# Attention and mixture of experts: the second products of the jobs of 448 and 360 columns change from row form to column form

## The chip, the cores and the metric

The program runs on one core of one Trainium2 chip. The metric is the device time of one launch in microseconds. The kernel before takes 369.8 us, the median of three runs (368.93 to 370.06).

## The reference

A gated linear attention gives one row of 384 values for each of 3072 tokens. A gate sends each token to one of eight experts, and each expert is a network of two layers. The change touches only the experts:

```python
expert_idx = np.argmax(x @ w_gate, axis=1)
...
h = np.maximum(np.einsum('ecd,edf->ecf', disp, w1), 0.0)
y = np.einsum('ecf,efd->ecd', h, w2)
...
out[i] = gate_w[i] * y[expert_idx[i], pos[i]]
```

Here D is 384 and F is 1024, so that one expert has a first product of 384 by 1024 and a second of 1024 by 384.

## The kernel before

The first 145 us or so are the attention. Its rows go to a scratch tensor in HBM, `disp`, sorted by expert. Then nine jobs run one after the other. Jobs 0 and 1 are the tokens of expert 0 (256 and 224 of them). Jobs 2 to 8 are the other experts, sorted by their number of tokens and padded to fixed sizes. In the branch that this input takes, the sizes are `T_USUAL`: 448, 424, 408, 392, 376, 360 and 352. A second branch with larger sizes (`T_SORTED`) is in the program and doesn't run.

Every job multiplies in pieces: an operand is split into a high part (`hh`, `xh`, `w1h`, `w2h`) and a rest (`hl`, `xl`, `w1l`, `w2l`), and three matmuls, high by high, rest by high and high by rest, make one product. The steps of a job are:

- `load_rows` (L1188, L1192) brings the job's rows `xg` from `disp`. `columns` (L1199) splits their words into two planes of 16 bits on POOL (L1206) and ACT (L1207), and SP issues one DMA transpose for each block of 128 rows (L1210), which gives `xq`. `prep_columns` (L1215) puts the planes together again (L1219 on POOL, L1220 on ACT) as `x` and splits `x` into `xh` (ACT, L1224) and `xl` (DVE, L1225). One buffer of `xh` and `xl` serves all jobs.
- `ffn1` (L1289) is the first product: for each of eight `ft`, nine matmuls (L762) with the job's T columns moving, into one bank of PSUM. `hidden_out` evicts it as `hh` (ACT, L768) and `hl` (DVE, L769).
- the second product has two forms. **Row form**, `ffn2_rows` (L1013): for each block of 128 tokens, 24 matmuls (L1023) whose stationary operand is 128 (or fewer) tokens of `hh` or `hl`, and whose moving operand is the 384 columns of `w2`. A last block of 64 tokens moves 384 columns too. ACT evicts each block with the gate as scale (`yo`, L1027), and POOL scatters its rows to the output (L334). **Column form**, `ffn2` (L1304): for each `ft` and each of three groups of 128 output features, three matmuls (L1312) whose stationary operand is `w2` and whose moving operand is the T tokens; three banks of PSUM fill together. Their result has features on the partitions, so ACT (L1318) and DVE (L1319) evict it as two planes of 16 bits, `yp`, and SP issues three DMA transposes to `yq` (L1320). In the first product of the next job, `emit_out` (L1326) puts the words together (POOL, L1332, and ACT, L1333), multiplies by the gate (ACT, L1334) and scatters.
- the weights of the next job are loaded by SP into a ring of three buffers (`raw`, L129 and L133) and split by ACT (L140) and DVE (L149; four pieces of job 2 on POOL).

`IN_ROWS` (L67) names the jobs whose second product is in row form. The rest of the loop decides by it too: after a job in row form `hook` is `None`, after one in column form it is the call of `emit_out`. Two more places hang on it:

```python
        nc.gpsimd.memset(yp[:, :, :, min(sizes[j - 2] for j in range(2, NE + 1) if j not in IN_ROWS) :], 0)
...
            if j == len(jobs) - 1:
                with tc.issue_after(out_ins[-1]):
                    nc.gpsimd.drain()
```

The second (L1373 to L1375) issues a drain of POOL behind the last scatter that `out_ins` knows. Only `ffn2_rows` appends to `out_ins`; the scatters of `emit_out` don't.

In the jobs from 2 on, the scheduler of the framework orders the instructions of each engine, from the dependences, the order of the code and its own model. Each engine takes its queue in order; SP's queue issues the loads and the transposes.

Of the kernel before, what the change touches and what calls it, by code (L numbers as in the profile page):

```python
# [29 lines left out]
def kernel(  # L30
# [33 lines left out]
    T_SORTED = (480, 440, 424, 408, 396, 384, 368)  # L64
    T_USUAL = (448, 424, 408, 392, 376, 360, 352)
    TMAX = max(T_SORTED)
    IN_ROWS = (0, 1, 2, 7, 8)  # L67
    NS = NE - 1
    XW = 2 * D + NE
    TOK0 = 4096  # L70
# [942 lines left out]
    def ffn2_rows(wt, hs, pr, T, fpool, hooks=None, fills=True):  # L1013
        w1h, w1l, w2h, w2l = wt
        gate, ti = pr[2:]
        for kb in range(-(-T // P)):
            n = min(P, T - kb * P)
            ks = slice(kb * P, kb * P + n)
            py = psM.tile([P, DM], F32, name="psM")
            for ft in range(FT):  # L1020
                hh, hl = hs[ft][:2]
                for m, (x, a) in enumerate(((hh, w2h), (hl, w2h), (hh, w2l))):
                    nc.tensor.matmul(py[:n], x[:, ks], a[:, ft], start=(ft == 0 and m == 0), stop=(ft == FT - 1 and m == 2))  # L1023
                if hooks and (kb, ft) in hooks:
                    hooks[kb, ft]()
            yo = fpool.tile([P, DM], F32, name="yo", bufs=2 if hooks and fills else 3)
            nc.scalar.activation(yo[:n], py[:n], AF.Copy, scale=gate[:n, kb : kb + 1])  # L1027
            with tc.issue_after(filling[-1]) if hooks and fills and kb else ExitStack():
                out_ins.append(scatter(out, ti[:n, kb : kb + 1], yo[:n], N - 1, ("out",)))
# [145 lines left out]
    def sorted_jobs(fctx, sizes):  # L1175
# [23 lines left out]
        def columns(xg, T):  # L1199
            nb, full = -(-T // P), T // P  # L1200
            planes = fpool.tile([P, 4, 2, DM], U16, name="planes", bufs=1)
            xq = fpool.tile([P, 2 * DT, whole(T_SORTED[1])], U16, name="xq", bufs=1)
            words = xg.bitcast(U16)[:, :, : 2 * DM].rearrange("r k (d w) -> r k d w", w=2)
            for r, ks in ((P, slice(0, full)), (whole(T - full * P), slice(full, nb))):
                if ks.start < ks.stop:
                    nc.gpsimd.tensor_copy(planes[:r, ks, 0], words[:r, ks, :, 1])  # L1206
                    nc.scalar.activation(planes[:r, ks, 1], words[:r, ks, :, 0], AF.Copy)  # L1207
            for kb in range(nb):
                r = whole(min(P, T - kb * P))
                nc.sync.dma_start_transpose(  # L1210
                    xq[:, :, kb * P : kb * P + r], planes[:r, kb].rearrange("r w d -> r (w d)")
                )
            return (xq,) + gates(xg, nb, fpool)
# [131 lines left out]
        yp = fpool.tile([P, DT, 2, 4 * P], U16, name="yp", bufs=1)  # L1345
        nc.gpsimd.memset(yp[:, :, :, min(sizes[j - 2] for j in range(2, NE + 1) if j not in IN_ROWS) :], 0)
        xgs, made = {}, {}
# [17 lines left out]
        for j, (_, T, ws) in list(enumerate(jobs))[2:]:  # L1365
# [15 lines left out]
            if j + 2 in xgs:  # L1381
                made[j + 2] = columns(xgs.pop(j + 2), jobs[j + 2][1])
            if j in IN_ROWS:
                ffn2_rows(wsets[ws], hs, cur, T, fpool)
# [207 lines left out]
```

## Time and profile before

| | |
|---|---|
| median of three runs | 369.8 us |
| the profiled execution, its own time | 366.9 us |
| its span, first to last instruction | 365.2 us |
| TensorE clock granted, mean | 0.997 |
| busy PE, DVE, ACT, POOL | 97%, 68%, 61%, 46% of the span |
| instructions | 10100 |

The profiled execution is one run, and its own time lies 0.8% below the median of the timed runs. Busy shares are averages over the attention and the experts. A matmul in the rows lasts about twice the distance to the next one, since two overlap; a price is therefore taken from the starts.

### The profile page before, as it was taken

What the parts mean: (1) busy time and instruction counts of PE and PEld (TensorE: products, weight loads), DVE (VectorE), ACT (ScalarE), POOL (GpSimd) and SP (SyncE); (2) the same over time, 40 slices, a digit from 0 to 9 for tenths busy, and PEclk for the clock granted to TensorE, in tenths of its full rate; (3) what the DMA queues carried; (4) which work ended last, traced back from release to release, by engine and by line L of the source; (5) the groups of instructions that cost most, each with busy time, mean ns of one, the idle gap of its engine ahead of it and who ended that gap; (6) DMA issues with size and microseconds to landing.
All of it is one profiled execution on the core that took longest, in us unless ns stands there. A gap on an engine that the chain in (4) does not pass through costs nothing. (4 is left out here: it accounts for less than half of the span.)

```text
span 365.2 us, 10100 instructions
## 1 busy us (share of the span) xinstructions
PE 355.5 (97%) x3895; PEld 335.1 (92%) x3895; DVE 247.2 (68%) x538; ACT 221.6 (61%) x457; POOL 166.8 (46%) x282
## 2 busy tenths in 40 slices
PE   7999999999999999999999999999999999999993
PEld 7999988888788889999999899999999999999993
DVE  4899997988798866745884576874954956670300
ACT  3356677886686754144677494868758776782310
POOL 6655555585767676241735320314615425073012
PEclk9999999999999999999999999999999999999998
DMA  8999999999999432467396779899599799831001
GB/s 149 197 174 218 216 192 232 244 217 203 230 222 245 132 114 90 135 217 229 115 253 225 194 245 214 254 230 278 162 205 275 173 193 292 167 124 61 14 23 43
DMA packets 110571, 67.54 MB, mean 185 GB/s; under 512 B 92996, under 2 KB 105053, under 8 KB 110513
## 3 DMA queue, kind: packets, MB, share of 16 engines
q1 hardware_dynamic: 106784, 56.74, 70.7%
q0 software_dynamic: 3456, 9.96, 7.9%
q8 instruction: 32, 0.52, 0.7%
q14 instruction: 27, 0.21, 0.2%
q10 hardware_dynamic: 272, 0.10, 0.1%
HBM read 49.26 MB, written 11.21 MB: 166 GB/s over the span
## 5 line engine op out<-in xcount | busy, mean ns | idle before, releaser
L334 POOL DMA_INDIRECT out_dram<-yo,g_ti x29 | 29.8, 1029 | 62.1 <-ACT yo L1027 43.8
L442 POOL TENSOR_SCALAR_AFFINE_SELECT AT<-AT 128x512 f32<-128x512 f32 x48 | 29.5, 640 | 21.0 <-ACT AT L440 20.9
L1023 PE MATMUL psM<-w2h,hh 128*128 128x384 f32 (+3 forms) x112 | 37.7, 341 | 0.0
L1023 PE MATMUL psM<-w2h,hl 128*128 128x384 f32 (+3 forms) x112 | 37.5, 338 | 0.0
L1023 PE MATMUL psM<-w2l,hh 128*128 128x384 f32 (+3 forms) x112 | 37.4, 337 | 0.0
L149 DVE TENSOR_TENSOR w2l<-raw,w2h 128x768 fp32r<-128x768 f32 x28 | 29.6, 1061 | 9.9 <-ACT w2h L140 9.4
L1312 PE MATMUL psM<-hh,w2l 128*128 128x424 f32 (+3 forms) x96 | 33.1, 345 | 0.0
L1312 PE MATMUL psM<-hl,w2h 128*128 128x424 f32 (+3 forms) x96 | 33.0, 344 | 0.0
L1312 PE MATMUL psM<-hh,w2h 128*128 128x424 f32 (+3 forms) x96 | 33.0, 344 | 0.0
L140 ACT ACTIVATE w2h<-raw 128x768 fp32r<-128x768 f32 x32 | 26.7, 842 | 9.6 <-DMA raw<-in_moe_w_dram 8.9
L394 DVE TENSOR_TENSOR_SCAN Suf<-psF,direv 112x511 f32<-112x511 f32 x24 | 29.1, 1210 | 4.5 <-PE psF L374 4.4
L440 ACT ACTIVATE AT<-psA 128x512 f32<-128x512 f32 x48 | 26.4, 613 | 8.9 <-PE psA L434 4.9
L1332 POOL COPY yo<-yq 128x384 uint16<-128x384 uint16 (+4 forms) x15 | 12.7, 898 | 38.4 <-DMA yq<-yp 36.5
L769 DVE SCALAR_TENSOR_TENSOR hl<-psA,hh 128x448 fp32r<-128x448 f32 (+8 forms) x24 | 13.0, 542 | 25.2 <-ACT hh L768 18.9
L434 PE MATMUL psA<-qT,kT 48*128 48x128 f32 x384 | 29.7, 293 | 0.0
L334 POOL DMA_INDIRECT disp<-rows,ri x24 | 24.9, 1036 | 10.1 <-issue 4.3
L408 DVE TENSOR_TENSOR_SCAN Rq<-psF,d 112x512 f32<-112x512 f32 x24 | 29.4, 1224 | 0.0
L140 ACT ACTIVATE w1h<-raw 128x1024 fp32r<-128x1024 f32 x24 | 25.2, 1058 | 4.2 <-DMA raw<-in_moe_w_dram 4.0
L149 DVE TENSOR_TENSOR w1l<-raw,w1h 128x1024 fp32r<-128x1024 f32 x21 | 25.7, 1231 | 2.9 <-ACT w1h L140 2.8
L434 PEld LDWEIGHTS psA<-qT,kT 48*128 48x128 f32 x384 | 26.1, 201 | 0.5 <-issue 0.5
L567 ACT ACTIVATE rows<-psA 128x384 f32<-128x384 f32 x24 | 11.8, 492 | 24.3 <-PE psA L551 18.5
L530 PE MATMUL psY<-AT,ld_v 128*48 128x128 f32 (+1 forms) x384 | 26.0, 273 | 0.0
(270 smaller groups left out, 1033.5 us busy)
## 6 DMA issues: line engine op xcount, KB each, us to landing
raw<-in_moe_w_dram SPq DMA_DIRECT2D x24, 512.0 KB
raw<-in_moe_w_dram SPq DMA_DIRECT2D x32, 384.0 KB
ld_kq<-in_k_dram SPq DMA_DIRECT2D x24, 192.0 KB
ld_kq<-in_q_dram SPq DMA_DIRECT2D x24, 192.0 KB
ld_v<-in_v_dram SPq DMA_DIRECT2D x24, 192.0 KB
ld_f<-in_f_logit_dram SPq DMA_DIRECT2D x11, 384.0 KB
xg<-disp SPq DMA_DIRECT2D x4, 589.5 KB
xg<-disp SPq DMA_DIRECT2D x5, 393.0 KB
```

Of the source, the lines that this page charges most:

```text
L140: return nc.scalar.activation(hi, raw, AF.Copy)
L149: engine.tensor_tensor(lo[cs], raw[cs], hi[cs].bitcast(F32), op=ALU.subtract)
L334: ins = nc.gpsimd.indirect_dma_start(out=dst, out_offset=bass.IndirectOffsetOnAxis(ap=idx, axis=0), in_=rows, in_offset=None, bounds_check ...
L394: nc.vector.tensor_tensor_scan(out=_view(Suf[:R], m - 1, [[-1, m]]), data0=_view(F, m, [[-1, m]]), data1=_view(direv[:R], m - 1, [[-1, m]] ...
L408: nc.vector.tensor_tensor_scan(out=Rq[:R], data0=F, data1=d1[:R], initial=0.0, op0=ALU.mult, op1=ALU.max)
L434: nc.tensor.matmul(pas[s][:, p], kTs[n][r, p], qTs[n][r, p], start=True, stop=True)
L440: nc.scalar.activation(AT[:, s], pas[s], AF.Copy)
L442: nc.gpsimd.affine_select(AT[:, s], AT[:, s], pattern=[[0, NP], [1, C]], compare_op=ALU.is_ge, fill=0.0, base=0, channel_multiplier=-1)
L530: nc.tensor.matmul(py[b][64 * g : 64 * g + m, a, :], vt[:, 2 * p + s, :m], AT[:, s, p, :], start=(first(n) and a == 0), stop=(a == NP // 2 ...
L769: nc.vector.scalar_tensor_tensor(out=hl[:, :T], in0=ph[:, :T], scalar=0.0, in1=hh[:, :T].bitcast(F32), op0=ALU.max, op1=ALU.subtract)
L1023: nc.tensor.matmul(py[:n], x[:, ks], a[:, ft], start=(ft == 0 and m == 0), stop=(ft == FT - 1 and m == 2))
L1312: nc.tensor.matmul(pys[c][:, :T], a[:, ft, cs], x[:, :T], start=(ft == 0 and n == 0), stop=(ft == FT - 1 and n == 2))
```

## The change

`IN_ROWS` loses jobs 2 and 7. The second product of job 2 (448 tokens) and of job 7 (360 tokens) is then made by `ffn2`, and evicted and scattered by way of `yp`, `yq` and `emit_out`. Jobs 0, 1 and 8 stay in row form.

```diff
     TMAX = max(T_SORTED)
-    IN_ROWS = (0, 1, 2, 7, 8)
+    IN_ROWS = (0, 1, 8)
     NS = NE - 1
```

By L1346 the part of `yp` that is set to zero once begins at column 360 and not at 376. By L1374 the drain of POOL is issued behind the last scatter of job 1 and not of job 7: in the built program it stands directly behind the scatter of job 1's second block, ahead of the fourth `w2l` on POOL.

The ACT queue from the conversion of job 3's rows (`x`, 424 columns) to the first evictions of job 3 (`hh`), before:

```order
L1220 ACTIVATE x_9230<-xq 128x3x424
L1027 ACTIVATE yo<-psM,g_gate 128x384
L1207 ACTIVATE planes<-xg 128x3x384
L1207 ACTIVATE planes<-xg 32x384
L1027 ACTIVATE yo<-psM,g_gate 128x384
...
L140 ACTIVATE w2h<-raw_3470 128x768
L1224 ACTIVATE xh<-x_9230 128x424 x3
L140 ACTIVATE w2h<-raw_3471 128x768
L140 ACTIVATE w2h<-raw_3469 128x768
L1027 ACTIVATE yo<-psM,g_gate 128x384
L140 ACTIVATE w2h<-raw_3470 128x768
L1027 ACTIVATE yo<-psM,g_gate 64x384
```

The same stretch with the change:

```order
L1220 ACTIVATE x_9239<-xq 128x3x424
L1207 ACTIVATE planes<-xg 128x3x384
L1207 ACTIVATE planes<-xg 32x384
...
L140 ACTIVATE w2h<-raw_3470 128x768
L1224 ACTIVATE xh<-x_9239 128x424 x3
L1318 ACTIVATE yp<-psM 128x448
L140 ACTIVATE w2h<-raw_3471 128x768
L1318 ACTIVATE yp<-psM 128x448
L140 ACTIVATE w2h<-raw_3469 128x768
L1318 ACTIVATE yp<-psM 128x448
L140 ACTIVATE w2h<-raw_3470 128x768
```

The four row evictions are gone, two of them from ahead of `xh`, and three pieces of job 3's `w2h` now stand between the column evictions.

SP's queue from the last piece of job 3's `w2` to the first of job 4's `w1` (L129), before:

```order
L133 DMA raw_3470<-in_moe_w_dram 128x2x384
...
L1210 DMA_TRANSPOSE xq<-planes 128x6x128 x3
L1210 DMA_TRANSPOSE xq<-planes 128x6x32
L1188 ISA
L1188 DMA xg<-disp 128x3x393
L1192 ISA
L1192 DMA xg<-disp 16x393
L129 ISA
L129 DMA raw_3471<-in_moe_w_dram 128x1024
```

and with the change:

```order
L133 DMA raw_3470<-in_moe_w_dram 128x2x384
...
L1320 DMA_TRANSPOSE yq<-yp 128x8x128
L1210 DMA_TRANSPOSE xq<-planes 128x6x128 x3
L1210 DMA_TRANSPOSE xq<-planes 128x6x32
L1320 DMA_TRANSPOSE yq<-yp 128x8x128 x2
L1188 ISA
L1188 DMA xg<-disp 128x3x393
L1192 ISA
L1192 DMA xg<-disp 16x393
L129 ISA
L129 DMA raw_3471<-in_moe_w_dram 128x1024
```

The three transposes of job 2's result stand around those of job 4's rows, ahead of the load of job 5's rows and of all weights of job 4.

## Rows read from the trace of the kernel before

**Rows 1.** The page, part 1: busy time, share of the span and instructions of each engine.

```profile
PE 355.5 (97%) x3895; PEld 335.1 (92%) x3895; DVE 247.2 (68%) x538; ACT 221.6 (61%) x457; POOL 166.8 (46%) x282
```

**Rows 2.** Busy time by stretch: job 3's first product, then its second; columns in the first line.

```profile
core 0: us, PE busy (x) PEld busy (x) DVE busy (x) ACT busy (x) POOL busy (x), PEclk, DMA share, GB/s
...
206.00:220.00 14.00, 14.00 (x75) 13.64 (x74) 8.66 (x19) 10.03 (x16) 4.26 (x5) 1.00 0.75 223
220.00:234.00 14.00, 14.00 (x75) 13.64 (x74) 9.29 (x19) 9.05 (x14) 3.57 (x4) 1.00 1.07 261
```

**Rows 3.** Line 1023 in job 2, row form: count, duration ns min/median/max, first and last start.

```profile
L1023 PE MATMUL psM<-w2h,hh x32: 332/333/342, 189.0 to 205.3; 128*128 128x384 f32 x24, 128*64 128x384 f32 x8
...
L1023 PE MATMUL psM<-w2l,hh x32: 333/338/342, 189.3 to 205.7; 128*128 128x384 f32 x24, 128*64 128x384 f32 x8
```

**Rows 4.** Line 1312 in job 3, column form of 424 columns.

```profile
L1312 PE MATMUL psM<-hh,w2h x24: 352/353/358, 219.7 to 233.0; 128*128 128x424 f32 x24
...
L1312 PE MATMUL psM<-hh,w2l x24: 349/357/362, 220.1 to 233.4; 128*128 128x424 f32 x24
```

**Rows 5.** Line 762 in job 7, first product of 360 columns, first and last group.

```profile
L762 PE MATMUL psA<-xh,w1h x9: 320/324/330, 310.9 to 320.7; 128*128 128x360 f32 x9
...
L762 PE MATMUL psT<-xh,w1l x9: 322/326/328, 312.7 to 322.5; 128*128 128x360 f32 x9
```

**Rows 6.** ACT in order of time around job 2's second product: start us, us, what.

```profile
191.78 1.67 ACT L1220 ACTIVATE x<-xq 128x1272 uint16<-128x1272 uint16 x1 [0.95 <-DMA xq<-planes]
195.87 0.58 ACT L1027 ACTIVATE yo<-psM,g_gate 128x384 f32<-128x384 f32 x1 [2.42 <-PE psM L1023]
...
199.26 1.44 ACT L1224 ACTIVATE xh<-x 128x424 fp32r<-128x424 f32 x3
```

**Rows 7.** DVE in order of time: job 3's last xl, job 4's last w1l.

```profile
201.62 0.56 DVE L1225 TENSOR_TENSOR xl<-x,xh 128x424 fp32r<-128x424 f32 x1
...
218.59 1.22 DVE L149 TENSOR_TENSOR w1l<-raw,w1h 128x1024 fp32r<-128x1024 f32 x1
```

**Rows 8.** SP in order of time: job 4's w1, the transposes of job 3's result.

```profile
208.74 1.52 SPq L129 DMA_DIRECT2D raw<-in_moe_w_dram  x3
...
237.90 5.00 SPq L1320 DMA_TRANSPOSE yq<-yp  x3
```

**Rows 9.** The instructions that read or write yq: duration ns min/median/max.

```profile
L1333 ACT ACTIVATE yo<-yq x15: 610/627/651, 245.0 to 322.0; 128x384 uint16<-128x384 uint16 x11, 40x384 uint16<-40x384 uint16 x1, 24x384 uint16<-24x384 uint16 x1, 8x384 uint16<-8x384 uint16 x1
L1332 POOL COPY yo<-yq x15: 615/628/1650, 245.1 to 321.3; 128x384 uint16<-128x384 uint16 x11, 40x384 uint16<-40x384 uint16 x1, 24x384 uint16<-24x384 uint16 x1, 8x384 uint16<-8x384 uint16 x1
```

**Rows 10.** Line 1375, POOL's drain: duration ns min/median/max, first and last start.

```profile
L1375 POOLq DRAIN  x1: 5687/5687/5687, 336.1 to 336.1; - x1
```

**Rows 11.** POOL in order of time, job 8.

```profile
336.33 1.01 POOL L334 DMA_INDIRECT out_dram<-yo,g_ti  x1 [2.97 <-ACT yo L1027]
...
360.59 0.94 POOL L334 DMA_INDIRECT out_dram<-yo,g_ti  x1 [3.20 <-POOLq L1554]
```

**Rows 12.** The page, part 5: the scatters to the output and to the scratch tensor.

```profile
L334 POOL DMA_INDIRECT out_dram<-yo,g_ti x29 | 29.8, 1029 | 62.1 <-ACT yo L1027 43.8
...
L334 POOL DMA_INDIRECT disp<-rows,ri x24 | 24.9, 1036 | 10.1 <-issue 4.3
```

**Rows 13.** Line 1588, the end of the program, POOL's part.

```profile
L1588 POOLq EVENT_SEMAPHORE  x4: 17/17/17, 364.4 to 365.1; - x4
L1588 POOLq DRAIN  x3: 50/107/368, 363.1 to 364.9; - x3
```

**Rows 14.** POOL in order of time where job 2 begins.

```profile
181.12 0.95 POOL L334 DMA_INDIRECT out_dram<-yo,g_ti  x1 [0.16 <-issue]
182.08 1.87 POOL L149 TENSOR_TENSOR w2l<-raw,w2h 128x768 fp32r<-128x768 f32 x1
183.87 1.61 POOL L1206 COPY planes<-xg 128x1152 uint16<-128x1152 uint16 x2
```

**Rows 15.** The instructions that read raw, from 170 us on: DVE's rests of w2.

```profile
L149 DVE TENSOR_TENSOR w2l<-raw,w2h x24: 942/959/2430, 199.5 to 327.5; 128x768 fp32r<-128x768 f32 x24
```

## The prediction

> **What bounds the kernel now.** I read the page's busy times first: PE is busy 97% of the span, the next engine 68% [rows 1]. An average over attention and experts says little, so the second view is the busy time by stretch. In job 3's first product PE is busy 14.00 of 14 us at full clock, and in its second product again, while ACT is busy 10.03 and 9.05 of them and DVE 8.66 and 9.29 [rows 2]. So from job 2 on the time is the number of matmuls times their distance, as long as operands come early enough. The DMA engines are the ones to watch: their mean busy share is 0.75 in the first stretch and 1.07 in the second (over 1, so the count lets packets overlap) [rows 2]. The third view is the tail: after the last matmul come one eviction, one scatter at 360.59 and the end of the program [rows 11, 13].
>
> **What PE saves.** In row form job 2 makes four blocks of 24 matmuls, 96 in all. They start from 189.0 to 205.7, which is 95 distances of 0.176 us: 16.9 us [rows 3]. The last block has 64 tokens and its matmuls are as far apart as the others. In column form there are 72 matmuls of 448 columns. No row shows a second product of 448, so I scale the nearest: job 3's 72 start from 219.7 to 233.4, 0.193 us apart for 424 columns, or 0.455 ns a column [rows 4]; 448 columns are then 0.204 us, and 72 of them 14.7 us. Job 2 saves 2.2 us. Job 7 makes 72 matmuls in either form. In row form they are 0.176 us apart [rows 3]; with 360 columns the first product of the same job has 71 distances between 310.9 and 322.5, 0.163 us each [rows 5]. It saves 72 times 0.0125, 0.9 us by these two rows; if a column costs the same 0.455 ns at 360 as at 424, the distance is 0.164 and the saving 0.85. I take 0.8, since the starts are given to a tenth of a us. Together 3.0 us, between 2.8 and 3.2.
>
> The Trainium skill (TensorE: Matmul & The Clock Gate, Back-to-back issue gap) gives an isolated gap of N/2.4 + 2.5 ns at the full clock. By it the two jobs would save 2.0 and 0.7 us, an estimate of 2.7 in place of 3.0. The rows show larger gaps (176 ns at 384 columns, where the page gives 162), and they decide.
>
> **What is added beside PE.** Per job: six evictions of `yp`, three transposes, then for each block of tokens one POOL copy and two ACT operations, against one ACT eviction for each block. A POOL copy takes 0.63 us and an ACT one 0.63 [rows 9]. Job 2 has four blocks, so ACT gets some 5 us more in job 3's first product, in which it is idle for 4 [rows 2]; its four row evictions of 0.58 [rows 6] are gone from the stretch before. PE doesn't feel ACT being late by two or three us there, because the column form asks for `hh` one `ft` at a time, nine matmuls or 1.7 us apart. For the same reason the weights' pieces that now stand between the column evictions on ACT are early enough. I cost all of this at nothing, and say below what it costs without that cover.
>
> On SP three transposes of a result hold the queue for 5.0 us [rows 8]. In job 3 they stand ahead of all weights of job 4. Job 4's last `w1l` is ready at 219.8 now [rows 7], and job 4 begins 0.2 us behind the last start of job 3, at 233.6 [rows 4]: a lead of 13.8 us. Of it go 2.2 (PE is earlier) and 5 (SP), and 6.6 remain. In job 8 the transposes have no load behind them. Nothing on the path.
>
> **Job 3's start** has the smallest lead. Its last `xl` ends at 202.2 [rows 7] and its first matmul follows the last of job 2 at 205.9 [rows 3], a lead of 3.7 us. With the shorter product 1.5 remain. Two row evictions of 0.58 leave the ACT queue ahead of `xh`, one of which waited 2.42 us for PE [rows 6], so `xh` may come earlier by 1.2 to 3.6 us, unless the next rows' `planes` then wait for their load. That makes a lead of 2.7 to 5.1.
>
> **The drain.** This is the term that I am least sure of. The drain is now issued where job 2 begins. Before, it stood in job 8 and took 5.69 us from 336.1 on [rows 10]; the scatter ahead of it ended at 337.3 [rows 11], so the drain alone took 4.4 us. Nothing waited for it: POOL had no work then. The program's last drain began at 363.1 and took 0.37 us [rows 13], and POOL went on at 364.4 only, so it had 0.9 us to spare. Ahead of the long one were 53 scatters (29 and 24 [rows 12], three that fill, less the last three), between it and the short one three. If a drain pays for the scatters since the last one, it is 4.4/53, 0.083 us each. The new first drain then has 31 behind it and takes 2.6 us; the last has 25, takes 2.1 in place of 0.37, and ends 1.7 us later. Less the 0.9 to spare, **the end comes 0.8 us later**. The bounds are 0 (a last drain is always short) and 4.4 us (it takes 5.69, less 0.37 and 0.9). I take 0.8, as the only value that holds for both rows.
>
> The first drain delays POOL's fourth `w2l` and job 3's `planes`, which followed the scatter at 182.1 and 183.9 [rows 14]. 2.6 us of delay in `planes` go through the transposes to `x` and `xh`, against a lead of 2.7 to 5.1. So nothing, just.
>
> **The sum.** -3.0 + 0.8 = -2.2 us on the profiled execution's own 366.9, which gives 364.7. The median of the timed runs is 369.8; 0.6% less is **367.6 us**.
>
> **The rivals.**
>
> *The last drain is free.* Then the gain is all of 3.0 us: 366.8. For it speaks that a program's last drain is a different one from a drain in the midst of work; against it, that only the number of scatters tells the two rows apart.
>
> *Job 3 starves.* If the new drain keeps POOL as long as the old one did, 4.4 us, or also waits for the landing of its scatter while the weights load, `xh` is late by up to 2 us beyond its lead. PE then waits about 2 us at job 3's first product: -2.2 + 2.0, 369.6, no difference. For it speaks that this lead is the shortest I found; against it, that the scheduler begins job 3 with five banks side by side, which asks for the second and third part of `xl` later.
>
> *The tail pays for the whole drain.* If the last drain takes the 5.69 us of the old one, the program ends 4.4 us later and the change is **slower**: -3.0 + 4.4 = +1.4, 371.2. It decides from a last drain of 4.3 us on (3.0 saved, 0.9 to spare, 0.37 there already). For it speaks that no other POOL drain behind many scatters is in the trace; against it, that fewer scatters lie behind the last drain now than lay behind the long one.
>
> *DVE and POOL block each other in jobs 3 and 4.* POOL's copies of `yq` reach 1.65 us where the median is 0.63 [rows 9], and DVE's `w2l` reaches 2.43 where it is 0.96 [rows 15]. Four copies and four rests, each about 1.2 longer, are 9.6 us; against the 6.6 left of job 4's lead that is a stall of 3.0, so -2.2 + 3.0 = +0.8, 370.6. Against it: they are the extremes, and DVE is idle for 5 us in that stretch [rows 2]. The Trainium skill (SBUF — State Buffer, SBUF: two separate sides) has it as a rule: a VectorE instruction with two SBUF inputs and a GpSimd one that reads SBUF hold the shared ports for a whole instruction. The extremes of rows 9 and 15 agree with it.
>
> That the change doesn't do what it says is out: the rows show the sizes 448 and 424, so the branch of `T_USUAL` runs.
>
> **How the numbers follow.** My forecast has 0.48, the free drain 0.12, job 3's starving 0.18, the tail 0.13, the blocking 0.09. What a measurement of this kernel can tell from no change is 0.3%, 1.1 us. Faster by more: nearly all of the first two, 0.59. The same: most of job 3's starving and the slow end of the forecast, 0.20. Slower: the tail, most of the blocking, the worst of job 3, 0.21. The range goes from 366.2, the free drain with the upper saving and a timing's spread, to 370.7, where it holds the blocking and leaves out the tail. The forecast's own range is 366.4 to 368.8.
>
> **What would show it.** Line 1312 should have 144 more matmuls, 72 of 448 columns 0.204 us apart and 72 of 360 columns 0.163 to 0.164 apart, and PE should go from job 2 to job 3 without a gap. Line 1375 should show the drain near 182 us with a duration between 2 and 3 us, and the last POOL drain of line 1588 one of about 2. I am wrong if PE is idle before line 762 of job 3 or 4 by over 1 us, if the drains' durations don't follow the number of scatters, or if the last POOL drain ends over 2 us later behind its scatter than now.

## The result: 1.05% slower

The change takes 372.5 us, the median of 14 runs (369.5 to 377.4); the kernel before takes 368.1 beside it (14 runs, 366.6 to 370.1). The ratio is 1.0105, with a 95% interval of 1.0074 to 1.0137. A second measurement gave 1.0171 (1.0112 to 1.0231). The forecast was 367.6 us, against 369.8 for the kernel before, so 0.6% faster, with a range from 366.2 to 370.7. Some runs of a kernel are slower, at a lower granted clock: the ratios leave them out, and since the profiled executions of `e8`, `e12` and the change's second measurement are such runs, only their waits, leads and stages are used and not their spans.

The profiled execution takes 374.9 us, its span is 373.2 us (365.2 before) and its mean granted clock 0.984. The end of the attention moves between profiled executions: job 2's second product begins at 189.0 us in the kernel before, at 190.9 with the change and between 186.6 and 194.1 in the experiments, though the code ahead is the same. So I compare **the stretch** from the first matmul of job 2's second product to the end: 176.2 us before, 182.3 with the change. By stage, from the starts of the first matmuls and of the last scatter:

| us | job 2, second product | job 3 | job 4 | job 5 | job 6 | job 7 | job 8 to last scatter | tail | stretch |
|---|---|---|---|---|---|---|---|---|---|
| before | 16.85 | 27.76 | 26.82 | 25.73 | 24.73 | 24.31 | 25.40 | 4.60 | 176.2 |
| change | 17.01 | 29.36 | 26.78 | 25.73 | 28.54 | 23.61 | 25.40 | 5.89 | 182.3 |
| change, drain late (below) | 14.73 | 27.76 | 26.82 | 25.73 | 24.74 | 23.61 | 25.40 | 4.47 | 173.3 |

The product itself is as forecast. These are the matmuls of line 1312 in job 2 and in job 7 (duration ns min/median/max, first and last start):

```profile
L1312 PE MATMUL psM<-hh,w2h x24: 367/368/368, 190.9 to 205.0; 128*128 128x448 f32 x24
...
L1312 PE MATMUL psM<-hh,w2l x24: 362/362/367, 191.3 to 205.4; 128*128 128x448 f32 x24
...
L1312 PE MATMUL psM<-hh,w2h x24: 324/325/327, 330.1 to 341.4; 128*128 128x360 f32 x24
...
L1312 PE MATMUL psM<-hh,w2l x24: 326/328/328, 330.4 to 341.8; 128*128 128x360 f32 x24
```

448 columns are 0.204 us apart (71 distances in 14.5 us), 360 columns 0.165. What came back lies elsewhere: PE stops twice. The groups of PE's matmuls around 207 and around 298 us (busy us, mean ns, then the idle time ahead and what ended it):

```profile
L762 PE MATMUL psA<-xh,w1h 128*128 128x424 f32 x3 | 1.7, 582 | 2.1 <-ACT xh L1224 2.1
...
L762 PE MATMUL psM<-xh,w1h 128*128 128x376 f32 x6 | 2.5, 414 | 1.9 <-DVE yp L1319 1.9
```

The first is job 3's start, which waits for `xh`; the second lies in job 6's first product, where a bank of `psM` isn't free because job 5's result has not been evicted. Behind each stop the granted clock falls. Busy time by stretch, with the two stretches of [rows 2] first:

```profile
core 0: us, PE busy (x) PEld busy (x) DVE busy (x) ACT busy (x) POOL busy (x), PEclk, DMA share, GB/s
...
206.00:220.00 14.00, 12.10 (x55) 11.70 (x56) 10.75 (x22) 9.81 (x20) 2.01 (x3) 0.88 0.59 141
220.00:234.00 14.00, 14.00 (x75) 13.63 (x74) 9.32 (x18) 10.51 (x20) 8.30 (x11) 1.00 0.76 234
...
299.00:311.00 12.00, 11.43 (x57) 11.09 (x58) 8.61 (x15) 8.84 (x19) 2.88 (x5) 0.86 0.97 186
```

The mean of 0.88 lies between the two levels, 1.2 and 2.4 GHz, so a part of the stretch ran at the lower one. The first matmuls of job 3 last 0.58 us and not 0.35.

**The drain.** Line 1375 and POOL in order of time where job 2 begins, answering to [rows 10] and [rows 14]:

```profile
L1375 POOLq DRAIN  x1: 10987/10987/10987, 179.4 to 179.4; - x1
```

```profile
183.03 0.95 POOL L334 DMA_INDIRECT out_dram<-yo,g_ti  x1 [0.16 <-issue]
190.55 2.49 POOL L149 TENSOR_TENSOR w2l<-raw,w2h 128x768 fp32r<-128x768 f32 x1 [6.58 <-ACT hh L768]
192.97 2.60 POOL L1206 COPY planes<-xg 128x1152 uint16<-128x1152 uint16 x2
```

POOL does nothing from 183.98 to 190.55. The row puts that down to ACT's `hh`, which is only the last semaphore that the profile saw; the drain, an instruction of the sequencer that isn't counted as busy, lasts from 179.4 to 190.4 and spans the gap. Its record begins ahead of the scatter, so its price is the gap and not the 10.99 us. Behind it `w2l` comes 6.6 us and `planes` 7.2 us later than in [rows 14], counted from the scatter. Why so long, the scatter's own record tells:

```profile
L334 POOL DMA_INDIRECT out_dram<-yo,g_ti x1: 947/947/947, 183.0 to 183.0; - x1
...
DMA to landing us min/median/max: 6.0/6.0/6.0
```

It takes 0.95 us on POOL, and its data land 6.0 us after it began, at 189.07, 1.3 us ahead of the drain's end. In that time the 16 DMA engines carry `xg` and the first weights of job 3 (mean 198 GB/s from 182 to 191). The Trainium skill (Perfetto Trace Analysis, DMA Instruction — SWDGE (GPSIMD)) says that the end of such a record is the end of descriptor making and not of the transfer; this trace agrees, with 0.95 against 6.0 us.

From `planes` the delay goes on to SP, which issues job 3's transposes behind them and the load of job 4's rows behind the transposes, and so to ACT:

```profile
202.19 1.66 ACT L1220 ACTIVATE x<-xq 128x1272 uint16<-128x1272 uint16 x1 [4.26 <-DMA xq<-planes]
204.84 1.58 ACT L1207 ACTIVATE planes<-xg 128x1152 uint16<-128x1152 uint16 x2 [1.00 <-DMA xg<-disp]
...
207.30 1.43 ACT L1224 ACTIVATE xh<-x 128x424 fp32r<-128x424 f32 x3
```

`x` is there at 203.85, but on ACT the `planes` of job 4's rows stand ahead of `xh` and wait for their load.

The last drain, which answers to [rows 13]:

```profile
L1588 POOLq EVENT_SEMAPHORE  x4: 17/17/17, 372.4 to 373.1; - x4
L1588 POOLq DRAIN  x3: 50/107/2161, 370.2 to 372.9; - x3
```

It takes 2.16 us (2.1 forecast), and the tail from the last scatter's start to the end is 5.89 us in place of 4.60.

### The profile page after: what moved, and what is told of

Same layout as the page of the kernel before. It is cut to its first block, busy times and chain, and to the rows that moved or that the text cites. A ratio compares the mean times of both kernels' runs of the same rounds, so it can differ in the third digit from the quotient of the medians.

```text
span 373.2 us, 10100 instructions
## 1 busy us (share of the span) xinstructions
PE 353.9 (95%) x3871; PEld 331.0 (89%) x3871; DVE 250.3 (67%) x544; ACT 224.1 (60%) x470; POOL 170.3 (46%) x289
## 5 line engine op out<-in xcount | busy, mean ns | idle before, releaser
L1312 PE MATMUL psM<-hh,w2l 128*128 128x448 f32 (+5 forms) x144 | 49.7, 345 | 0.0
L1312 PE MATMUL psM<-hl,w2h 128*128 128x448 f32 (+5 forms) x144 | 49.6, 345 | 0.0
L1312 PE MATMUL psM<-hh,w2h 128*128 128x448 f32 (+5 forms) x144 | 49.5, 345 | 0.0
L1332 POOL COPY yo<-yq 128x384 uint16<-128x384 uint16 (+6 forms) x22 | 14.6, 712 | 41.8 <-DMA yq<-yp 39.5
L140 ACT ACTIVATE w1h<-raw 128x1024 fp32r<-128x1024 f32 x24 | 25.1, 1056 | 10.8 <-DMA raw<-in_moe_w_dram 10.8
L434 PE MATMUL psA<-qT,kT 48*128 48x128 f32 x384 | 27.7, 281 | 2.0 <-ACT parts L577 1.5
L1312 PEld LDWEIGHTS psM<-hh,w2l 128*128 128x128 f32 x144 | 27.0, 188 | 0.6
L1312 PEld LDWEIGHTS psM<-hh,w2h 128*128 128x128 f32 x144 | 27.0, 188 | 0.5
L1312 PEld LDWEIGHTS psM<-hl,w2h 128*128 128x128 f32 x144 | 27.0, 188 | 0.5
L434 PEld LDWEIGHTS psA<-qT,kT 48*128 48x128 f32 x384 | 24.2, 189 | 2.9 <-ACT parts L577 1.7
L762 PE MATMUL psA<-xh,w1h 128*128 128x448 f32 (+6 forms) x63 | 22.7, 361 | 2.1 <-ACT xh L1224 2.1
```

Of the source, the lines that this page charges most:

```text
L140: return nc.scalar.activation(hi, raw, AF.Copy)
L434: nc.tensor.matmul(pas[s][:, p], kTs[n][r, p], qTs[n][r, p], start=True, stop=True)
L762: nc.tensor.matmul(ph[:, :T], a[:, c, fs], x[:, c, :T], start=(n == 0), stop=(n == 3 * DT - 1))
L1312: nc.tensor.matmul(pys[c][:, :T], a[:, ft, cs], x[:, :T], start=(ft == 0 and n == 0), stop=(ft == FT - 1 and n == 2))
L1332: nc.gpsimd.tensor_copy(words[:n, :, 1], yq[:n, 0, kb])
```

## Experiments

The first question was whether the early drain makes both stops (theory D) or the column form itself makes the second (theory T). Later runs set theory O, on SP's order, against D.

| kernel | ratio to before (95%) | stretch us | stop at job 3 | stop at job 6 | tail us |
|---|---|---|---|---|---|
| change | 1.0105 (1.0074 to 1.0137) | 182.3 | 2.1 | 1.9 | 5.9 |
| change, second measurement | 1.0171 (1.0112 to 1.0231) | 186.0 | 4.2 | 2.9 | 5.6 |
| `e1`: drain late | 0.9961 (0.9922 to 1.0001) | 173.3 | 0 | 0 | 4.5 |
| `e1`, second measurement | 0.9930 (0.9884 to 0.9976) | 173.4 | 0 | 0 | 4.6 |
| `e2`: no drain | 1.0040 (0.9992 to 1.0087) | 177.0 | 0 | 0 | 8.2 |
| `e3`: before, drain early | 1.0101 (1.0040 to 1.0162) | 181.5 | 2.4 | 0 | 5.7 |
| `e5`: job 2 alone | 0.9966 (0.9924 to 1.0008) | 173.8 | 0 | 0 | 4.3 |
| `e6`: job 7 alone | 0.9992 (0.9945 to 1.0039) | 176.1 | 0 | 0 | 5.2 |
| `e8`: drain behind the planes | 0.9908 (0.9863 to 0.9953) | 174.3 | 0 | 0 | 5.5 |
| `e9`: drain behind `w2l` | 1.0030 (0.9981 to 1.0079) | 174.6 | 0 | 0 | 5.5 |
| `e11`: second weight piece behind `yp` | 1.0140 (1.0073 to 1.0207) | 179.5 | 1.9 | 2.2 | 5.8 |
| `e12`: loads ahead of the result | 1.0087 (1.0037 to 1.0136) | 180.5 | 4.2 | 0 | 5.7 |
| `e13`: drain late, loads ahead | 0.9850 (0.9793 to 0.9907) | 173.2 | 0 | 0 | 4.4 |

### The drain late (`e1`, measured twice)

```diff
-                scatter(out, ti[:n, kb : kb + 1], yo[:n], N - 1, ("out",))
+                out_ins.append(scatter(out, ti[:n, kb : kb + 1], yo[:n], N - 1, ("out",)))
...
-                with tc.issue_after(out_ins[-1]):
-                    nc.gpsimd.drain()
+                emit = hook[1]
+
+                def emit_and_drain():
+                    emit()
+                    with tc.issue_after(out_ins[-1]):
+                        nc.gpsimd.drain()
+
+                hook = hook[0], emit_and_drain
```

> The change with the drain of POOL put back to where it stood before, in job 8, here behind the last scatter of job 7's column form. Theory D (the early drain holds POOL until its scatter has landed, so job 3's rows come late, PE stops for 2.5 us at job 3, the clock falls, and the lost lead makes the second stop of 2.2 us at job 6): both stops go, the last drain of POOL takes 0.2 to 0.4 us again, and the run is 2.0 to 3.0 us faster than the kernel before (ratio 0.992 to 0.995). Theory T (the transposes and the loads of the column form themselves make ACT wait for the weights' buffers): the stop at job 3 goes, the one at job 6 stays, and with it 3.8 us: ratio 1.001 to 1.005.

> The change with the late drain once more, to narrow the interval of the first measurement (0.9922 to 1.0001): a stretch of 173.3 us and a ratio of 0.990 to 0.997.

No stop, and every stage as forecast (table above). POOL in order of time, at the place of the change's drain:

```profile
178.92 0.95 POOL L334 DMA_INDIRECT out_dram<-yo,g_ti  x1 [0.16 <-issue]
179.87 1.86 POOL L149 TENSOR_TENSOR w2l<-raw,w2h 128x768 fp32r<-128x768 f32 x1
181.99 1.59 POOL L1206 COPY planes<-xg 128x1152 uint16<-128x1152 uint16 x2 [0.26 <-DMA xg<-disp]
```

This scatter too lands 6.0 us after its start, and nobody waits for it. The stretch is 2.9 us shorter than before. The ratio of the first measurement is nearer to 1 than that gives (0.992) and just includes 1.000; the second excludes it. Theory T falls: both jobs are in column form and there is no stop at job 6.

### No drain (`e2`)

```diff
-            if j == len(jobs) - 1:
-                with tc.issue_after(out_ins[-1]):
-                    nc.gpsimd.drain()
```

> The change without the drain in the midst of the program. Theory D: no stop at job 3 or at job 6, as in the run with the late drain. The last drain of POOL then has all 56 scatters behind it. If a drain pays 0.083 us for each scatter since the last one, it takes 4.7 us in place of 0.37 and the tail is 3.4 to 4.4 us longer than that of the kernel before, so the ratio is 1.000 to 1.005. If a last drain costs the same however many scatters are behind it (2.16 us, as in the change), the ratio is 0.995 to 0.998. Theory T: the stop at job 6 stays and the run is 3.8 us slower than either.

No stop either. The last drain (here line 1585) has all 56 scatters behind it:

```profile
L1585 POOLq DRAIN  x3: 44/107/4713, 359.8 to 365.1; - x3
```

4.71 us, where 56 times 0.083 is 4.65. The tail is 3.6 us longer than before. So the drain in the midst is worth having: it takes the scatters' price off the tail.

### The drain alone, in the kernel before (`e3`)

```diff
+        job1_scatter = out_ins[-1]
...
-                with tc.issue_after(out_ins[-1]):
+                with tc.issue_after(job1_scatter):
                     nc.gpsimd.drain()
```

> The kernel before, rows form throughout, with the drain alone moved to where the change has it, behind the last scatter of job 1. Theory D: the drain holds POOL for 9 to 11 us, until its scatter has landed; job 3's rows are late by some 8 us against a lead of 3.7, so PE stops for 2 to 5 us at job 3, and the tail pays 1.3 us more as in the change: 3 to 9 us slower than before (ratio 1.008 to 1.025). Theory T: without the column form there is neither the stop at job 6 nor the long wait at job 3: at most the 1.3 us of the tail, ratio 1.002 to 1.005.

The move of the drain, with nothing else, makes the first stop:

```profile
L1376 POOLq DRAIN  x1: 11477/11477/11477, 175.2 to 175.2; - x1
```

```profile
L762 PE MATMUL psA<-xh,w1h 128*128 128x424 f32 x4 | 2.1, 533 | 2.4 <-ACT xh L1224 2.4
```

Job 2's second product and job 3 take 2.6 and 1.6 us more than before, the tail 1.1, in sum 5.3 us. Job 6 takes 24.74 us as before. So the early drain makes the first stop, its slow clock and the longer tail, but not the stop at job 6 by itself.

### Job 2 alone (`e5`) and job 7 alone (`e6`)

```diff
-    IN_ROWS = (0, 1, 8)
+    IN_ROWS = (0, 1, 7, 8)
```

> Job 2 alone in column form, job 7 in row form; the drain stays behind job 7's last scatter. Theory D: no stop, job 2 saves 2.2 us, tail as in the kernel before: 1.5 to 2.5 us faster (ratio 0.993 to 0.996). Theory T: the three transposes of job 2's result in job 3 set the weights late, a stop of about 2 us with a lower clock follows in jobs 4 to 6: ratio 1.000 to 1.006.

For job 7 alone the line reads `(0, 1, 2, 8)`.

> Job 7 alone in column form, job 2 in row form. The drain then stands behind job 2's last row scatter, in job 3, ahead of the conversion of job 4's rows. Theory D: POOL is held there for 31 plus 4 scatters' price or until the scatter lands, 3 to 7 us, against a lead of job 4's rows of 10 us: no stop. Job 7 saves 0.7 us, the tail costs about 1.0 us (21 scatters behind the last drain): the stretch from job 2's second product to the end is 176.2 to 176.8 us and the ratio 0.998 to 1.004. If a drain early in the jobs costs wherever it stands: 179 us or more, ratio above 1.006.

Job 2 alone shortens the stretch by 2.4 us with the drain in its old place; its ratio, 0.9966, lies just above the 0.993 to 0.996 expected. Job 7 alone gains 0.7 us in job 7 and loses 0.6 in the tail. Its drain begins at 204.3 us and takes 5.3; what it holds, POOL's half of job 4's `x`, comes at 210.2 and isn't due before job 4 begins, at 231.2. There is no stop in either, as theory D has it, and neither ratio can be told from no change.

### The drain a few instructions on (`e8`, `e9`)

`e8` issues the change's drain behind the two `planes` of job 3, `e9` behind POOL's last `w2l`, one instruction behind the scatter (the lists `planes_ins` and `pool_low`, new in these kernels, name those instructions):

```diff
-                with tc.issue_after(out_ins[-1]):
+                with tc.issue_after(planes_ins[1]):
                     nc.gpsimd.drain()
```

```diff
-                with tc.issue_after(out_ins[-1]):
+                with tc.issue_after(pool_low[-1]):
                     nc.gpsimd.drain()
```

> The change, with its early drain moved three instructions on in POOL's queue: behind the last w2l and the two planes of job 3, where POOL has no work for some 6 us. The queues of ACT, DVE, SP and PE are those of the kernel with the late drain. The stretch from the first matmul of job 2's second product to the end is 176.2 us before, 182.3 with the change and 173.3 with the late drain. Theory D (the drain costs only what stands behind it on POOL): no stop at job 3 or at job 6; the last drain has 25 scatters behind it and takes 2.16 us, so the tail is 1.3 us longer: 174.6 us, ratio 0.996 to 1.001. Rival E (a drain this early costs wherever it stands, since it waits for the DMA engines while the weights load): 179 us or more.

> The early drain moved one instruction on: behind POOL's last w2l and ahead of the planes of job 3. The ring of weight buffers is then not held up, the rows of job 3 still are. Theory D: the drain ends 1.3 us after its scatter lands, some 7 us after the scatter is issued, so the planes come 4 to 6 us late against a lead of 3 to 4: PE stops for 1 to 2.5 us at job 3, the third weights of job 3 come in time, and the stretch from job 2's second product to the end is 176 to 179 us. If instead the held ring (and not the rows) made the stop of the change, there is none and the stretch is 174.6 us.

`e8` has no stop and a stretch of 174.3 us (174.6 expected): not the drain's earliness costs, but what stands behind it. Its ratio, 0.991, is below the 0.996 to 1.001 expected; the stretch alone gives 0.995. POOL of `e9` in order of time, and ACT a little later:

```profile
190.97 1.74 POOL L1208 COPY planes<-xg 128x1152 uint16<-128x1152 uint16 x2 [5.05 <-issue]
```

```profile
205.13 1.44 ACT L1226 ACTIVATE xh<-x 128x424 fp32r<-128x424 f32 x3
```

In the change the planes come at 192.97 and `xh` at 207.30; both profiles have the scatter at 183.0 to 183.1 and job 2's second product at 190.9, so they may be compared directly. Held for 5.1 us, without the 2.5 us of `w2l` ahead, the planes are 2.0 us earlier, `xh` is 2.2 us earlier, and PE begins job 3 at 205.73 without a gap, as soon as the first part of `xh` is ready. My expected stop of 1 to 2.5 us did not show. No stop and a stretch of 174.6 us is what the other theory on record forecast, that the held ring of weight buffers, and not the rows, made the stop. The change's own trace speaks against it:

```profile
182.22 11.18 SPq L129 DMA_DIRECT2D raw<-in_moe_w_dram  x3
194.15 5.34 SPq L1210 DMA_TRANSPOSE xq<-planes  x4
```

The load that waits for the ring has left SP at 193.40, and the transposes of job 3's rows go out only at 194.15, when the first `planes` on POOL is done (192.97 and 1.15 us): the rows end the wait. Counted from the scatter, the `xh` of `e9` comes 3.9 us later than in the kernel before, as much as the lead in which it may be late (3.9 us, below). So the held rows use up the lead, and the `w2l` behind the drain turns that into a stop. The profile stands on the edge, though, and the timed runs (ratio 1.003, where the stretch gives 0.996) don't bear it out; that they do stop for a while is likely, and not shown.

### What makes the stop at job 6 (`e11`, `e12`)

ACT of the change in order of time ahead of the second stop:

```profile
292.54 1.04 ACT L140 ACTIVATE w1h<-raw 128x1024 fp32r<-128x1024 f32 x1
296.73 1.06 ACT L140 ACTIVATE w1h<-raw 128x1024 fp32r<-128x1024 f32 x1 [3.14 <-DMA raw<-in_moe_w_dram]
297.69 0.60 ACT L1334 ACTIVATE yo<-yo,g_gate 24x384 f32<-24x384 f32 x1
298.20 1.22 ACT L1318 ACTIVATE yp<-psM 128x392 uint16<-128x392 uint16 x3
```

A piece of job 7's `w1` waits 3.14 us for its load, with job 5's eviction behind it. `e11` puts the second piece behind the evictions, as the third is already:

```diff
-                for ins in evicted[-2:] if n == DT - 1 else ():
+                for ins in evicted[-2:] if n else ():
```

> The change with its early drain, and one order more: the second piece of the next job's w1 (ACT and DVE) is put behind the evictions of the job's result, as the third piece is already. Theory D says that the late loads reach PE at job 6 by one way alone: the conversion of job 7's second piece stands ahead of the eviction of job 5's result on ACT and waits for its load there. Then the stop at job 3 stays (2.5 us), the one at job 6 and its slow clock go, and the stretch from job 2's second product to the end falls from 182.3 to about 178.5 us, ratio to the kernel before 1.003 to 1.008. If the weights or the rows of job 6 are themselves too late, PE stops in job 6 or 7 all the same and the stretch stays above 181 us.

That theory fell. The stop stays and only changes its releaser: ACT's `hh` and DVE's `hl` of job 6 now stand behind the late pieces.

```profile
L762 PE MATMUL psA<-xh,w1h 128*128 128x376 f32 x6 | 2.1, 351 | 2.2 <-DVE hl L769 2.2
```

(The stretch of this profile, 179.5 us and not the 181 or more that I expected with a stop, is shorter since the clock did not fall behind either stop: 1.00 from 207 to 221 us and from 300 to 312. The timed runs are no faster than the change.) So the loads themselves are late. Their lead tells where: from the end of a job's last `w1l` to its first matmul, in us.

| | job 4 | job 5 | job 6 | job 7 |
|---|---|---|---|---|
| before | 13.8 | 21.4 | 21.7 | 19.8 |
| `e3`: before, drain early | 8.3 | 18.0 | 19.3 | 17.1 |
| `e1`: drain late | 4.8 | 10.8 | 19.0 | 18.6 |
| `e9`: drain behind `w2l` | 3.4 | 9.0 | 16.9 | 17.1 |
| change | 3.6 | 3.8 | 13.8 | 16.7 |
| `e12` | 7.1 | 15.4 | 19.3 | 17.6 |

In `e9` job 4's lead is as short as in the change, but job 5's is 5.6 us longer again; in the change it stays as short. SP's queue differs there. SP of the change in order of time at the start of job 4 (237.3 us):

```profile
240.46 4.53 SPq L1320 DMA_TRANSPOSE yq<-yp  x3
245.18 0.58 SPq L1188 DMA_DIRECT2D xg<-disp  x1
245.98 0.35 SPq L1192 DMA_DIRECT2D xg<-disp  x1
246.86 0.89 SPq L129 DMA_DIRECT2D raw<-in_moe_w_dram  x2
```

and of `e1`, where job 4 starts at 229.3:

```profile
229.02 0.38 SPq L1188 DMA_DIRECT2D xg<-disp  x1
229.65 0.34 SPq L1192 DMA_DIRECT2D xg<-disp  x1
230.54 0.35 SPq L129 DMA_DIRECT2D raw<-in_moe_w_dram  x1
231.10 1.49 SPq L1320 DMA_TRANSPOSE yq<-yp  x1
```

With the change the three transposes of job 3's result wait for their evictions ahead of job 6's rows and job 5's weights, and the first weight load is issued 9.6 us behind job 4's start in place of 1.2. Between the two programs only the drain moved, and the scheduler put SP, ACT and DVE in another order; why it chose that order isn't shown. `e3` and `e9`, whose drains are early too, have the rows and at least the first load ahead of the three transposes, as `e1` has, and no stop at job 6. `e2` and `e8` have the very order of `e1` on SP, ACT, DVE and POOL, so these three can't tell the held POOL from the order. `e12` keeps the early drain and sets that one point of SP's order by hand (the transposes are taken out of `ffn2` as `turn_out`):

```diff
                 load_weights(into, e, rawpool)
+                if turn_out is not None:
+                    with tc.issue_after(raws[-DT]):
+                        turn_out()
+                    turn_out = None
```

> The change with its early drain, and SP's queue set by hand in one point: the three transposes of a job's result stand behind the first weight load of the next job and not ahead of the rows and of all weights. Theory O (the stop at job 6 comes from the order that the scheduler made for SP once it saw the early drain: the transposes of job 3's result wait on SP for their evictions and hold the rows and the weights of job 5 back by some 7 us): job 5's weights are ready 9 us or more ahead of job 5, where the change had 3.8; the stop at job 3 stays (about 2 us), the one at job 6 is gone, and the stretch from job 2's second product to the end is 177.5 to 179 us; ratio to the kernel before 1.002 to 1.007. Theory D alone (the held POOL itself is what the jobs carry along): the lead of job 5 stays under 6 us, the stop at job 6 stays, and the stretch is 181 us or more.

> The change itself once more, on the chip of the three others, to see whether its two stops are the same in another profiled run: 2.1 and 1.9 us at jobs 3 and 6, a stretch of 181 to 183 us, ratio 1.007 to 1.014.

The stop at job 3 is there, of 4.2 us, and of 4.2 us as well in the change beside it, whose stop is that much longer than in its first profile; `e12` in the view of PE's groups:

```profile
L762 PE MATMUL psA<-xh,w1h 128*128 128x424 f32 x5 | 2.1, 416 | 4.2 <-ACT xh L1224 4.2
```

The stop at job 6 is gone (job 6 takes 24.74 us; 29.50 in the change beside it) and job 5's lead is 15.4 us. SP of `e12` where job 4 starts, at 239.2:

```profile
237.92 5.50 SPq L129 DMA_DIRECT2D raw<-in_moe_w_dram  x3
244.02 5.34 SPq L1323 DMA_TRANSPOSE yq<-yp  x3
```

The stretch is 180.5 us, above the 179 that I had set as the end for theory O because the first stop was longer, and 5.4 us under the change's. The timed runs point the same way (median 370.3 us of 12, 374.4 of 6 for the change beside it), though the two intervals meet and 1.0087 lies above the 1.007 expected. Theory O holds: with the drain as early as in the change, another order takes the second stop away. One reserve stays: the edit acts in every job from job 3 on, and moved instructions on ACT and DVE too, so the one point of SP's queue isn't shown to be enough by itself.

### Both repairs (`e13`)

`e12` with the drain of `e1`.

> Both repairs: the drain late, behind job 7's column form, and the transposes of a result behind the first weight load of the next job. Both theories expect no stop and the stretch of the kernel with the late drain alone, 173.3 us, within 0.4, since PE bounds it; only the leads of the weights should be longer (job 4's over 8 us where the late drain alone had 4.8). Ratio 0.990 to 0.995.

The stretch is 173.2 us and the lead of job 4 12.1 us. The median is 362.7 us against 367.1 before, and the ratio, 0.985, is below those of `e1` and `e12` and below the 0.990 to 0.995 expected. Its interval overlaps that of `e1`'s second measurement, and the stretches are equal, so a gain of the second repair over the first isn't shown. As with `e8` and `e9`, the ratio lies 0.4 to 0.7% from what the stretch gives, here 0.992.

## Why the prediction was wrong

- **What PE saves**: right. 3.0 us forecast (2.8 to 3.2); with the late drain 16.85 less 14.73 and 24.31 less 23.61, in sum 2.8, at the lower end. The estimate of 2.7 by the Trainium skill (TensorE: Matmul & The Clock Gate, Back-to-back issue gap) is as near, but its gap for 448 columns, 0.189 us, differs from the 0.204 measured here, and the measurement decides.
- **What is added beside PE, at nothing**: right. With the late drain no stage is longer than before.
- **SP's transposes, 6.6 us of job 4's lead left**: 4.8 in `e1`, 1.8 less, and it still held. The three transposes hold SP for 4.0 us there and not 5.0, so the loss beyond the price arose at another place, which isn't shown.
- **Job 3's lead, 2.7 to 5.1 us**: too high, measured as forecast from the end of the last `xl`: 1.6 to 3.1 us in the kernels with job 2's column form and no early hold (`e1` twice, `e2`, `e5`, `e8`, `e13`). The reserve that the prediction named came true, since the next rows' `planes` wait for their load (1.94 us in `e1`). But PE begins with the first part of `xh` alone. Before, that was ready 6.0 us ahead (worked out from [rows 6] and PE's start); less the 2.1 us by which the product is shorter, 3.9 remain (3.8 to 5.3 in those kernels).
- **The drain: here the step failed.** "The new first drain then has 31 behind it and takes 2.6 us", and so "2.6 us of delay in `planes`" and "nothing, just". The price of 0.083 us for each scatter is right, as `e2` shows at 56, but it is one of two conditions. The early drain also lasts until its scatter has landed, and that took 6.0 us with the DMA engines loading weights; it ends 1.3 us behind that, 6.4 us after the scatter's end, where 31 scatters would have made 2.6. POOL was held for 6.6 us, `planes` came 7.2 us later than in [rows 14] counted from the scatter, and `xh` 6.1: a stop of 6.1 less 3.9, 2.2 us. The rows held the warning: [rows 10, 11] come from a stretch without loads, and [rows 2] show the DMA engines busy while the jobs load.
- **The last drain**: 2.1 us forecast, 2.16 measured. The end came 1.3 us later and not 0.8, since the last drain began 0.4 us later behind its scatter. With that, all three signs of being wrong that the prediction names have come: PE idle for 2.1 us, a drain that doesn't follow the number of scatters, and a last drain that ends 2.15 us later behind its scatter.
- **The rival "Job 3 starves"** named the mechanism, landing included, and the stop of 2.0 us. It left out what follows: 1.6 us of lower clock behind the stop, and 3.8 us in job 6. The sum is -2.8 +2.2 +1.6 +3.8 +1.3 = +6.1 us of the stretch in the profiled execution (374.9 us, clock 0.984). The medians are only 4.4 us apart, and the two fastest runs of the change, 369.5 and 370.1 us, had a clock of 0.998: what the lower clock costs differs from run to run.
- **What no term had**: that SP's order differs in the jobs behind. I read it as far as the first load of job 4's weights, and the harm stood one job on.
- **DVE and POOL blocking each other**: the longest `w2l` of DVE is 2.75 us in the change and 3.42 in `e1`, but no stage in `e1` is longer than before.

## What to carry to other kernels

A drain of GpSimd costs what stands behind it in the queue: look up when the DMA ahead of it lands under the load of that place, and put the drain where the engine has no work for that long. Here three instructions on (`e8`) turned a loss of 6 us in the stretch into a gain of 2. A list like `out_ins`, filled by one branch and read by another, moves an instruction without any line of the diff saying so; and where a scheduler sets the order, one moved instruction can change another engine's queue two jobs later, so compare the whole order of the queue that feeds the bound.

## What the runs showed of the hardware

- The last drain of POOL: 0.37 us with 3 scatters since the drain before (0.38 to 0.65 in `e1` and `e13`), 1.83 with 21, 2.16 with 25, 4.71 with 56: 0.082 us for each scatter between the first and the last.
- A drain among loads ends 1.3 to 1.5 us behind the landing of its scatter: in the change (twice), `e3`, `e8`, `e9`, `e11` and `e12` with a landing 6.0 to 6.6 us after the scatter's start, and in `e6` with one of 3.6. It follows the transfer there, and not the number of scatters (31, and 35 in `e6`).
- The granted clock fell behind most of the stops of 1.9 to 4.2 us (0.88, 0.86 in the change) and not behind those of 1.9 and 2.2 us in `e11` (1.00). What decides stays open.
